# Sliding-window attention and a gated FFN on one core: casts on two engines, fillers for PE, token halves, later loads through POOL's queue

## The chip, the cores and the metric

The kernel runs on one core of a Trainium2 chip. The metric is the device time of one execution in microseconds (us); lower is better. The times below are the median of several executions, and one execution was recorded by the hardware profiler. PE is the matrix engine, DVE the vector engine, ACT the scalar engine, POOL the GpSimd engine, SP the engine that here only issues transfers (DMAs).

## The reference

For each of 8 batches and 8 heads, attention over 576 tokens of 64 numbers with a window of 32 to each side; then an FFN of 512 to 1024 to 512 with a convolution of three taps over the tokens and a gate.

```python
scores = scale * np.matmul(q, k.transpose(0, 1, 3, 2))
mask = np.abs(pos[:, None] - pos[None, :]) <= window          # window = 32
attn = softmax(np.where(mask, scores, -1e9))
x = np.matmul(attn, v)                                        # heads side by side: (8, 576, 512)
h = np.maximum(x @ w_in, 0.0)                                 # (8, 576, 1024)
conv_out = sum(conv_w[k] * h_shifted[k] for k in range(3))
out = (h * sigmoid(conv_out)) @ w_out                         # (8, 576, 512) float32
```

Inputs and output are float32; the kernel computes its products in bfloat16.

## The kernel before

The kernel does not run loops at run time: everything is laid out once as a list of tasks. `Order.add` takes a task with the engines that could do it, what it reads and writes, and a wanted time `t`. `Order.run` is a planner: it keeps a modelled clock for each engine and picks, again and again, the ready task with the smallest `t`; a task with two possible engines goes to the one that the model has done first. It emits each task as it is picked, so each engine's order of instructions is fixed by the planner. The wanted times come from `PARAMS`. PSUM has 8 banks; a task that opens banks waits until the planner finds some free.

The attention goes batch by batch (`loads`, `transposes`, `scores`, `values`, `x_turned`). `loads` brings q and k of a batch in two tiles each (`qkst`, 128 partitions by 1152 numbers) and V in five overlapping blocks (`vst`); POOL casts each to bfloat16 (`qkb`, `ve`), and DVE makes a copy of V shifted by 64 rows (`vo`). There is one set of staging tiles, and two sets of the cast ones. `paced` lets a load of batches 2 to 7 begin only when the load two before it has landed. `transposes` turns q and k on PE, ACT or DVE copy them out of PSUM (`qT`, `kT`); `scores` computes nine tiles of 64 by 128 per head, ACT takes the exponential, DVE multiplies by the mask; `values` multiplies with V and a column of ones, DVE divides by the sum (`rec`, `xn`); `x_turned` transposes the result into `xT`.

The FFN goes by chunks of 384 tokens: 12 chunks, three for each two batches. Chunk 0 lies in batch 0; chunk 1 holds the last 192 tokens of batch 0 and the first 192 of batch 1, and is done in two parts (`part` 0 and 1) so that the first can go ahead of batch 1. `first` is the product with w_in and the relu (`hT`), `moves` shifts slices of `hT` between partitions by SBUF-to-SBUF DMAs into `gT`, `gates` does the convolution by small products with diagonal blocks, tanh on ACT and the gating product on DVE, and `second` is the product with w_out, whose result goes through the tile `wst` to the output. The weights are loaded in float32 into that same tile and cast by POOL.

All loads, moves and stores are issued by SP in one queue, in the planner's order; only the small conv weights come through ACT. The beginning is ordered by wanted times far below zero: q, k and V of batch 0, w_in, q, k and V of batch 1, w_out.

Of the kernel before, what the change touches and what calls it, by code (L numbers as in the profile page):

```python
# [14 lines left out]
RING = 3100  # L15

# [15 lines left out]
class Order:  # L32
# [3 lines left out]
    def __init__(self):  # L36
        self.tasks, self.writer, self.readers = [], {}, {}

    def add(self, kinds, emit, t, reads=(), writes=(), opens=None, ps=(), after=(), claims=()):


        deps = set(after)
# [10 lines left out]
        task = Task(len(self.tasks), kinds, emit, t, deps, opens, ps)  # L53
        task.soft = soft - deps
        for k in reads:
            self.readers.setdefault(k, []).append(task)
# [8 lines left out]
    def run(self, emit=True):  # L65
        free = {"PE": 0.0, "ACT": 2800.0, "DVE": 6000.0, "POOL": 4400.0, "SP": 800.0}
        mode, channel, backlog = None, 0.0, []
        bank_free = [0.0] * 8
# [40 lines left out]
        while pending:  # L109
            best = None  # L110
            for e, xs in ready.items():
# [5 lines left out]
                while pick is None:  # L117
# [18 lines left out]
                    if pick is None:  # L136
                        later = min([later] + [x.ready for x in xs if x.ready > now])
                        if later == float("inf"):
                            break
                        now, held = later, []  # L140
                if pick and (best is None or pick[0] < best[0] - 1e-6):
                    best = (pick[0], e, pick[1], pick[2])
# [3 lines left out]
            if len(x.kinds) > 1:  # L146
                def done(k):
                    return max(free[k], x.ready) + x.kinds[k][1]
                f = min(x.kinds, key=done)
                if f != e:  # L150
                    e, now = f, max(free[f], x.ready)
                    busy, result, more = x.kinds[e]
            if e == "PE":
                if more != mode:
                    busy, result, mode = busy + 90.0, result + 90.0, more
            if e == "SP":
# [6 lines left out]
                channel = max(now + busy + 600.0, channel) + packets * each / 16.0  # L163
                backlog.append((channel, packets))
                result = channel + slack - now
            free[e] = now + busy
# [16 lines left out]
            for y in x.after:  # L183
                if x in y.deps:
                    y.ready = max(y.ready, x.end + (0.0 if e == "SP" else SEM))
# [9 lines left out]
def kernel(  # L195
# [68 lines left out]
    mask = sb([128, 2, S], BF16, "mask")  # L264

# [24 lines left out]
    def pl(n):  # L290
        return 150 + 0.85 * n, 200 + 0.85 * n, None
# [6 lines left out]

    def turn(s):
# [4 lines left out]
    o = Order()  # L304
    nc.scalar.dma_start(conv_w24, moe_conv_w.rearrange("k (m p) -> (k m) p", p=128))
# [32 lines left out]


# [8 lines left out]

    def loads(b):
        i = b % NLD  # L350

        def load_qk(y, j):
            src = (q, k)[y][b, 4 * j:4 * j + 4, :, :]
            sync.dma_start(
                qkst[y][j].rearrange("p e j d -> p e (j d)"),
                bass.AP(src.tensor, src.offset, [[RP * D, 128], [2 * S * D, 2], [1, RP * D]]),
            )

# [3 lines left out]
        def load_v(c):  # L362
            lo = 128 * c - PAD
            s0, s1 = max(0, lo), min(S, lo + 128)
            sync.dma_start(
# [14 lines left out]
        if b < 2:  # L380
            x, dx = (-100.0 if b == 0 else -50.0), 0.1
# [5 lines left out]
        def paced():  # L387
            return before[-2:-1] if b > 1 and len(before) > 1 else []

        for j in range(NPH):  # L390
            for y in range(2):
                t = x + n * dx
                o.add({"SP": dma(256, 110)}, lambda e, y=y, j=j: load_qk(y, j), t,
                      writes=[("st", y, j)], after=paced())
                before.append(o.tasks[-1])
                o.add({"POOL": pl(1152)}, lambda e, y=y, j=j: cast_qk(y, j, e), t,
                      reads=[("st", y, j)], writes=[("b", i, y, j)])
                n += 1
        for c in range(NBLK):
            t = x + n * dx  # L400
            o.add({"SP": dma(1024, 21)}, lambda e, c=c: load_v(c), t, writes=[("vst", c)], after=paced())
            before.append(o.tasks[-1])
            o.add({"POOL": pl(512)}, lambda e, c=c: cast_v(c, e), t,
                  reads=[("vst", c)], writes=[("ve", i, c)])
            n += 1
        for cs in ((0, 2), (2, 4)) if b == 0 else ((0, 4),):
            for half in range(2):
                o.add({"DVE": dve(520 * (cs[1] - cs[0]), 4)},
                      lambda e, cs=cs, half=half: shift(half, cs), x + n * dx,
                      reads=[("ve", i, c + half) for c in range(*cs)],  # L410
                      writes=[("vo", i, c, half) for c in range(*cs)])

    def load_w_in():
        for h in range(2):
# [9 lines left out]
            o.add({"SP": dma(512, 95)}, load, -60.0, writes=[("ws", 4 * h + c) for c in range(4)])  # L424
            for c in range(KC):
                o.add({"POOL": pl(512)}, lambda e, h=h, c=c: cast(e, h, c), -60.0 + h,
                      reads=[("ws", 4 * h + c)], writes=[("w_in", h, c)])

    def load_w_out():
        rows = moe_w_out.rearrange("(h c p) f -> p h c f", c=4, p=128)  # L430
        for c in range(4):
            def load(e, c=c):
                for lo, at, n in turn(c):
# [5 lines left out]
            o.add({"SP": dma(256, 95, len(turn(c)))}, load, -40.0,  # L439
                  writes=[("ws", 4 * h + c) for h in range(2)])  # L440
            for h in range(2):
                o.add({"POOL": pl(512)}, lambda e, h=h, c=c: copy(e, w_out_sb[:, 4 * h + c, :], ws[:, 4 * h + c, :]),
# [18 lines left out]
    def conv_weights():  # L461
        ps = Banks(1)
        o.add({"PE": pe(200.0, "f32")},
              lambda e: tensor.matmul(bank(ps, 0)[:, 0:3 * MB], conv_w24, ident24, start=True, stop=True),
              5.0, opens=ps, writes=[("cw24",)])
        o.add({"DVE": dve(24)}, lambda e: vector.tensor_copy(
            out=conv_w_sb.rearrange("p k m -> p (k m)"), in_=bank(ps, 0)[:, 0:3 * MB]),
            5.0, reads=[("cw24",)], writes=[("cw",)], ps=[ps])
        o.add({"DVE": dve(768)}, lambda e: vector.tensor_tensor(
# [5 lines left out]
    def transposes(g2):  # L475
# [3 lines left out]
        i, n = b % NLD, g2 % NKT  # L479
        for y in range(2):  # L480
# [16 lines left out]
            o.add({"PE": pe(280.0, "rows")}, mm, t + Q["TR"],  # L497
                  reads=[("b", i, y, j)], writes=[("tr", g2, y)], opens=ps,
                  claims=[("T", n, y, h) for h in range(2)])
            for h in range(2):  # L500
                o.add({"ACT": act(576), "DVE": dve(576)},
# [366 lines left out]
```

## Time and profile before

| | |
|---|---|
| three runs | 241.81, 242.25, 245.48 us; median 242.25 |
| the profiled execution | 243.37 us, span from first to last instruction 241.7 us |
| busy: PE, DVE, ACT, POOL | 208.1, 160.1, 164.0, 80.9 us |
| granted clock of PE, mean | 0.972 |
| DMA | 49.62 MB, mean 205 GB/s; the SP queue's packets took 71.6% of 16 engines' span |
| batch 0's first cast of q / first FFN product / first product with w_out | 4.76 / 25.54 / 54.62 us |

The span is what the trace covers; the execution's own time has some 1.7 us around it. Busy time counts an engine's instructions, without its waits and without the issuing of DMAs. A matrix product's recorded time includes its way through the array, so PE's busy share is not its share of peak. Line 274 of the kernel is the helper through which nearly all instructions go, so rows are told apart by their tiles.

### The profile page before, as it was taken

What the parts mean: (1) busy time and instruction counts of PE and PEld (TensorE: products, weight loads), DVE (VectorE), ACT (ScalarE), POOL (GpSimd) and SP (SyncE); (2) the same over time, 40 slices, a digit from 0 to 9 for tenths busy, and PEclk for the clock granted to TensorE, in tenths of its full rate; (3) what the DMA queues carried; (4) which work ended last, traced back from release to release, by engine and by line L of the source; (5) the groups of instructions that cost most, each with busy time, mean ns of one, the idle gap of its engine ahead of it and who ended that gap; (6) DMA issues with size and microseconds to landing.
All of it is one profiled execution on the core that took longest, in us unless ns stands there. A gap on an engine that the chain in (4) does not pass through costs nothing. (4 is left out here: it accounts for less than half of the span.)

```text
span 241.7 us, 9128 instructions
## 1 busy us (share of the span) xinstructions
PE 208.1 (86%) x3878; PEld 124.3 (51%) x3906; DVE 160.1 (66%) x268; ACT 164.0 (68%) x291; POOL 80.9 (33%) x96
## 2 busy tenths in 40 slices
PE   1536995589998869999999998999999999999993
PEld 0425464365655454565455654655555655555541
DVE  7586166998575899546399779698684595524140
ACT  1650586445698576679977886679778885876751
POOL 5757744536613444662236517321000000000000
PEclk9999999758999997999999999999999999999999
DMA  6999999989698899969489989756132223342534
GB/s 237 292 289 392 248 233 223 275 229 337 168 290 186 217 293 355 328 186 278 98 207 356 264 225 281 161 129 205 37 129 55 79 105 68 123 110 54 177 113 181
DMA packets 67228, 49.62 MB, mean 205 GB/s; under 512 B 46172, under 2 KB 52340, under 8 KB 67188
## 3 DMA queue, kind: packets, MB, share of 16 engines
q1 hardware_dynamic: 67152, 49.03, 71.6%
q8 instruction: 30, 0.49, 0.9%
q14 instruction: 10, 0.08, 0.1%
q10 hardware_dynamic: 36, 0.01, 0.0%
HBM read 32.52 MB, written 9.44 MB: 174 GB/s over the span
## 5 line engine op out<-in xcount | busy, mean ns | idle before, releaser
L274 PE MATMUL pst<-xT,w_in_sb 128*128 128x385 bf16 (+2 forms) x416 | 75.4, 322 | 1.6 <-ACT xT L274 0.6
L274 PE MATMUL pst<-w_out_sb,gT 128*128 128x512 bf16 x260 | 64.3, 384 | 3.2 <-issue 2.2
L274 PEld LDWEIGHTS <-w_in_sb 128*128 128x128 bf16 x416 | 37.6, 100 | 25.8 <-issue 3.4
L274 ACT ACTIVATE hT<-pst 128x385 bf16<-128x385 f32 (+2 forms) x80 | 38.6, 489 | 11.1 <-PE pst L274 10.1
L274 DVE SCALAR_TENSOR_TENSOR gT<-tn,gT 128x384 bf16<-128x384 f32 (+2 forms) x52 | 42.4, 842 | 3.9 <-DMA gT<-hT 3.9
L274 POOL CAST ve<-vst 128x512 bf16<-128x512 f32 x40 | 29.4, 741 | 45.7 <-DMA vst<-in_v_dram 43.5
L274 ACT ACTIVATE attn<-pst 128x640 bf16<-128x640 f32 x64 | 39.4, 667 | 4.9 <-PE pst L274 4.9
L274 PEld LDWEIGHTS <-gT 128*128 128x128 bf16 x288 | 26.6, 99 | 31.0 <-issue 3.3
L274 ACT ACTIVATE tn<-pst 128x768 f32<-128x768 f32 (+1 forms) x52 | 37.4, 768 | 6.5 <-PE pst L274 4.6
L274 ACT COPY wst<-pst 128x512 f32<-128x512 f32 x36 | 21.2, 588 | 29.6 <-PE pst L274 28.1
L274 DVE TENSOR_TENSOR attn<-attn,mask 128x1152 bf16<-128x1152 bf16 x32 | 26.9, 846 | 12.3 <-ACT attn L274 12.1
L274 DVE TENSOR_TENSOR xn<-pst,rec 128x640 bf16<-128x640 f32 x32 | 25.8, 818 | 0.5
L274 DVE SCALAR_TENSOR_TENSOR gT<-tn,hT 128x384 bf16<-128x384 f32 (+1 forms) x26 | 14.7, 564 | 16.5 <-ACT tn L274 16.4
L274 POOL CAST qb<-qst 128x1152 bf16<-128x1152 f32 x16 | 19.9, 1242 | 16.2 <-DMA qst<-in_q_dram 12.5
L274 POOL CAST kb<-kst 128x1152 bf16<-128x1152 f32 x16 | 19.9, 1243 | 16.0 <-DMA kst<-in_k_dram 14.3
L274 PE MATMUL pst<-hT,diag_w 32*32 32x384 bf16 (+1 forms) x1248 | 21.2, 322 | 1.8 <-DVE xn L274 1.0
L274 ACT COPY xT<-pst 128x1024 bf16<-128x1024 bf16 (+1 forms) x16 | 11.8, 781 | 13.9 <-PE pst L274 13.9
L274 PEld LDWEIGHTS <-attn 128*64 128x64 bf16 x640 | 14.1, 119 | 13.6 <-issue 8.6
L274 PE MATMUL pst<-ve,attn 128*64 128x65 bf16 x384 | 17.4, 206 | 3.8 <-DVE attn L274 2.3
L274 PE MATMUL pst<-qT,kT 64*128 64x64 bf16 x576 | 17.5, 197 | 3.1 <-DVE kT L274 0.8
L274 PE MATMUL pst<-vo,attn 128*64 128x65 bf16 x256 | 15.6, 206 | 3.3 <-DVE vo L274 3.3
L274 PEld LDWEIGHTS <-kT 64*128 64x128 bf16 x576 | 12.2, 98 | 12.0 <-issue 9.2
(37 smaller groups left out, 163.4 us busy)
## 6 DMA issues: line engine op xcount, KB each, us to landing
qst<-in_q_dram SPq DMA_DIRECT2D x16, 576.0 KB, 6.4
kst<-in_k_dram SPq DMA_DIRECT2D x16, 576.0 KB, 7.3
out_dram<-wst SPq DMA_DIRECT2D x11, 768.0 KB, 5.8
vst<-in_v_dram SPq DMA_DIRECT2D x24, 256.0 KB, 5.5
vst<-in_v_dram SPq DMA_DIRECT2D x16, 192.0 KB, 5.9
wst<-in_moe_w_in_dram SPq DMA_DIRECT2D x2, 1024.0 KB, 7.9
gT<-hT SPq DMA_DIRECT2D x14, 144.0 KB, 3.6
gT<-hT SPq DMA_DIRECT2D x34, 48.0 KB, 2.1
```

What stands on the lines that cost most here:

```text
L274: return lambda *args, **kwargs: fixed(do(*args, **kwargs))
```

## The change

- Casts of q, k, V, w_in and w_out may go to POOL or ACT; the planner picks whichever it has done first. In the planner POOL's casts, DVE's masks, shifts and gating products share a modelled port, so that it does not lay them over one another.
- Fillers: where the planner sees a gap ahead of a PE task before 62 us, `warm` issues products of a constant tile into PSUM bank 7, as many as fit; bank 7 is held back from other use until then.
- Token halves: batch 0 is loaded, cast, transposed, scored (tiles 0 to 3, then 4 to 8), masked, multiplied with V (blocks 0 and 1, then 2 to 4) and turned in two halves of tokens, and chunk 0 of the FFN is done in two parts. The order of loads becomes: first half of q and k (k through ACT's queue), V blocks 0 to 2, half of w_in, second half of q and k, V blocks 3 and 4, the other half of w_in, batch 1, w_out.
- q, k and V of batches 2 to 7 are issued by POOL, and `paced` looks four loads back.
- The planner's numbers (`PARAMS`) are other ones, and each task's wanted time gets an offset from a table (`NUDGE`, by kind of task and batch or chunk), so the order of the instructions is another one throughout.

The core of the diff:

```diff
     def run(self, emit=True):
...
+        bank_free = [0.0] * 7 + [WARM]
...
+            if e == "POOL" and isinstance(more, tuple):
+                packets, each, slack = more
+                second = max(now + busy + 1000.0, second, channel) + packets * each / 16.0
+                result = second + slack - now
...
+            if e == "PE" and emit and now < WARM:
+                gap, each = (now - free[e], 260.0) if free[e] else (now - 4000.0, 430.0)
+                self.warm(int((gap - 300.0) / each))
...
+    def load(b, packets, ns):
+        return {"POOL": (1000.0, None, (packets, ns, 1300.0))} if b > 1 else {"SP": dma(packets, ns)}
...
+    def warm(n):
+        for i in range(n):
+            tensor.matmul(pst[:, 7, :], warm_sb[:, 0:128], warm_sb, start=True, stop=True)
...
         def load_qk(y, j):
             src = (q, k)[y][b, 4 * j:4 * j + 4, :, :]
-            sync.dma_start(
+            (pool if b > 1 else sync).dma_start(
...
+        def load_half(y, j, half):
+            for e_ in range(2):
+                src = (q, k)[y][b, 4 * j + 2 * e_:4 * j + 2 * e_ + 2, 32 * RP * half:32 * RP * half + 32 * RP, :]
+                (scalar if y and not half else sync).dma_start(
+                    qkst[y][j][64 * e_:64 * e_ + 64, half, :, :].rearrange("p j d -> p (j d)"),
+                    bass.AP(src.tensor, src.offset, [[RP * D, 32], [S * D, 2], [1, RP * D]]),
+                )
...
         def paced():
-            return before[-2:-1] if b > 1 and len(before) > 1 else []
+            return before[-4:-3] if b > 1 and len(before) > 3 else []
...
-                o.add({"POOL": pl(1152)}, lambda e, y=y, j=j: cast_qk(y, j, e), t,
-                      reads=[("st", y, j)], writes=[("b", i, y, j)])
+                o.add("qc", {"POOL": pl(1152), "ACT": act(1152)}, lambda e, y=y, j=j: cast_qk(y, j, e), t,
+                      reads=[("st", y, j)], writes=[("b", i, y, j)] + [("b0", y, j, h) for h in halves0])
...
-        for i in range(NP):
-            values(b * NP + i)
+        for part in (0, 1) if b == 0 else (None,):
+            for i in range(NP):
+                values(b * NP + i, part)
```

296 lines of the change are left out of this document (205 added, 91 removed), and 79 rows, old and new, of tables (NUDGE, PARAMS).

## The prediction

> **What bounds the kernel now.** I began with the page: span, busy shares, and the row of PE in forty slices.
>
> ```profile
> span 241.7 us, 9128 instructions
> PE 208.1 (86%) x3878; PEld 124.3 (51%) x3906; DVE 160.1 (66%) x268; ACT 164.0 (68%) x291; POOL 80.9 (33%) x96
> PE   1536995589998869999999998999999999999993
> ```
>
> PE is thin in the first eight or nine slices and nearly full behind them. So the second view was the busy time by stage (stage, its length, busy us of PE, PEld, DVE, ACT, POOL, granted clock, DMA share, GB/s), cut at the first FFN matmul, at the two stretches with a lower clock, at the last loads and at the tail.
>
> ```profile
> 0.00:25.50 25.50, 10.83 (x246) 8.83 (x246) 17.75 (x43) 9.57 (x15) 17.40 (x27) 1.00 1.01 307
> 25.50:45.40 19.90, 15.91 (x344) 10.47 (x344) 11.06 (x21) 13.44 (x25) 11.40 (x16) 1.00 0.99 221
> 45.40:52.40 7.00, 4.49 (x108) 3.53 (x108) 6.71 (x12) 1.62 (x3) 2.41 (x2) 0.50 0.86 260
> 52.40:55.60 3.20, 3.20 (x62) 1.96 (x60) 2.39 (x8) 2.48 (x5) 1.22 (x2) 0.50 0.95 331
> 55.60:80.00 24.40, 22.80 (x496) 13.91 (x499) 17.78 (x27) 19.34 (x39) 10.92 (x12) 1.00 0.90 238
> 80.00:89.70 9.70, 6.86 (x185) 4.53 (x184) 9.03 (x15) 6.42 (x12) 4.47 (x5) 1.00 0.88 251
> 89.70:93.20 3.50, 3.17 (x24) 2.11 (x23) 3.44 (x4) 2.47 (x3) 2.09 (x3) 0.51 1.08 371
> 93.20:160.00 66.80, 64.42 (x1208) 37.29 (x1216) 47.94 (x77) 51.47 (x93) 28.38 (x30) 1.00 0.88 241
> 160.00:230.00 70.00, 68.63 (x1139) 38.15 (x1150) 41.79 (x68) 52.79 (x94) 2.58 (x3) 1.00 0.34 102
> 230.00:241.70 11.70, 7.82 (x81) 3.52 (x80) 2.24 (x4) 4.44 (x7) 0.00 (x0) 1.00 0.40 148
> ```
>
> Length minus PE busy gives PE's idle time: 14.7 + 4.0 + 2.5 = 21.2 us before 52.4, then 1.6, 2.8, 0.3, 2.4 and 1.4, and 3.9 in the tail: 33.6 in all. Three things follow. From 93.2 to 230 PE is busy 133.1 of 136.8 us: little is to be had there, and only by taking PE away from its work could it get worse. Before 52.4 PE does not bound; the DMA engines are full (1.01, 0.99) and DVE is. And between 80 and 89.7 DVE is busy 9.03 of 9.70 us while PE idles.
>
> The third view was the order of time around the early steps.
>
> ```profile
> 25.54 4.12 PE L274 MATMUL pst<-xT,w_in_sb 128*128 128x385 bf16 x16 [0.55 <-ACT xT L274]
> 27.74 0.15 PEld L274 LDWEIGHTS <-w_in_sb 128*128 128x128 bf16 x1 [0.17 <-issue]
> 28.06 1.20 PEld L274 LDWEIGHTS <-w_in_sb 128*128 128x128 bf16 x7 [0.17 <-issue]
> 18.90 2.29 POOL L274 CAST w_in_sb<-wst 128x512 bf16<-128x512 f32 x4 [1.43 <-DMA wst<-in_moe_w_in_dram]
> 34.57 0.62 POOL L274 CAST ve<-vst 128x512 bf16<-128x512 f32 x1 [1.53 <-DMA vst<-in_v_dram]
> 40.23 1.03 DVE L274 COPY vo<-ve 64x2080 bf16<-64x2080 bf16 x1
> 42.16 1.11 DVE L274 COPY vo<-ve 64x2080 bf16<-64x2080 bf16 x1
> 44.28 0.21 DVE L274 RECIPROCAL rec<-pst 128x10 f32<-128x10 f32 x1
> 44.52 0.82 DVE L274 TENSOR_TENSOR xn<-pst,rec 128x640 bf16<-128x640 f32 x1
> 49.78 1.67 PE L274 MATMUL pst<-ident,xn 128*128 128x128 bf16 x14 [0.85 <-DVE xn L274]
> 50.63 1.01 ACT L274 COPY xT<-pst 128x1024 bf16<-128x1024 bf16 x1 [4.80 <-PE pst L274]
> 52.46 1.48 PE L274 MATMUL pst<-xT,w_in_sb 128*128 128x193 bf16 x8
> 54.62 2.37 PE L274 MATMUL pst<-w_out_sb,gT 128*128 128x512 bf16 x7
> ```
>
> The first FFN matmul starts at 25.54. Weight loads of this group come 0.32 us apart at 27.74 and 1.20 / 7 = 0.17 apart from 28.06, so the array ran at half pace until then although the clock column says 1.00; I count all that lies before 28.06 as half pace. The landmark I use is 52.46, where chunk 1's second half, the first work that needs batch 1, reaches PE; behind it PE does not stop for long. Batch 1's last V block was cast at 34.57, 17.9 us earlier. The work between is short; it waits in DVE's queue behind the FFN of chunk 0 (the shifts start at 40.23 and 42.16).
>
> **The change part by part.**
>
> *Token halves, and casts on two engines.* Less has to land before the first FFN matmul: half of q and k, three of five V blocks and the first half of w_in are 1.2 + 0.7 + 1.0 MB where 3.5 + 1.0 MB landed by 18.90. At that pace (18.90 us less about 2 of start) it lands at 2 + 16.9 x 2.9 / 4.5 = 12.9; four casts by two engines take 1.2 us, so I expect the first FFN matmul near 16, with the first quarter of the work only. That alone moves nothing at the end: it clears chunk 0 from DVE and ACT before batch 1 arrives. The bytes ahead of batch 1's last V are the same, so it still lands near 34.5. From there: cast 0.6, two shifts 2.1, values about 0.5, four normalisations 4 x (0.21 + 0.82) = 4.1, turning 1.7, copy 1.0: 44.5. The landmark moves from 52.46 to between 44.5 and 52.46. I take 44.5, because chunk 0 is out of the way by then: gain **7.9**, bounds 0 and 8.
>
> The halves add instructions: eight extra issues on SP and four on ACT, 72 more transposes, four more masks, reciprocals and normalisations, eight more activations. At 0.2 to 0.5 us each these are some 3 us on DVE and 3 on ACT; in 0.00:25.50 these have 7.8 and 15.9 us free. Nothing is charged; without that cover it would be 3 us.
>
> *Work pulled forward.* The first w_out product starts at 54.62. With the chunk-0 gates done early, some of its 5 us can fill PE before the landmark, but only as w_out's casts allow:
>
> ```profile
> 42.11 3.27 POOL L274 CAST w_out_sb<-wst 128x512 bf16<-128x512 f32 x4 [1.39 <-DMA wst<-in_moe_w_out_dram]
> ```
>
> They end at 45.4 and cannot end much sooner with the DMA engines full. Gain 0 to 3, taken as **2**.
>
> *Fillers.* They occupy PE only in planned gaps up to 62 us, from a tile that nothing else uses. What they buy behind the landmark is the half clock of 52.40:55.60: PE was busy all 3.20 us at 0.50, so **1.6**. Before the landmark a faster array shortens only parts of a chain set by loads and DVE; I add nothing. Their price: one PSUM bank less until 62 us and a filler that runs past its gap, 0.43 us each by 512 columns at the pace above (0.32 us for 385). 0 to 2, taken as **-0.5**, one filler.
>
> *Between 80 and 93.2* PE loses 2.8 + 0.3 idle and 1.6 by the 0.51 clock. DVE limits there, and no DVE work is removed after batch 0. Another order may spread it: 0 to 4, taken as **1.5**.
>
> *Loads of batches 2 to 7 through POOL, four in flight.* Three rows bound what an issue costs.
>
> ```profile
> 52.11 0.46 SPq L274 DMA_DIRECT2D vst<-in_v_dram  x1
> 0.80 0.65 ACTq L305 DMA_DIRECT2D conv_w<-in_moe_conv_w_dram  x1
> 16.63 13.35 SPq L274 DMA_DIRECT2D vst<-in_v_dram  x5
> 165.46 0.82 POOL L274 CAST ve<-vst 128x512 bf16<-128x512 f32 x1 [2.02 <-DMA vst<-in_v_dram]
> 42.72 0.55 SPq L274 DMA_DIRECT2D qst<-in_q_dram  x1
> L274 POOL CAST ve<-vst 128x512 bf16<-128x512 f32 x40 | 29.4, 741 | 45.7 <-DMA vst<-in_v_dram 43.5 <-PE pst L274 1.3 <-DVE attn L274 0.7
> L274 POOL CAST kb<-kst 128x1152 bf16<-128x1152 f32 x16 | 19.9, 1243 | 16.0 <-DMA kst<-in_k_dram 14.3 <-PE pst L274 1.5
> L274 POOL CAST qb<-qst 128x1152 bf16<-128x1152 f32 x16 | 19.9, 1242 | 16.2 <-DMA qst<-in_q_dram 12.5 <-PE pst L274 3.7
> ```
>
> A V block's issue took 0.46 us when nothing held it, ACT's only one 0.65, and 13.35 / 5 = 2.67 where a full queue held it. The trace has no issue by POOL. I take 1.0, near the low rows because four in flight do not fill a queue; bounds 0.46 and 2.67. The loads of six batches span 42.72 to 165.46, 20.5 us a batch, or some 18.8 when 10 us are saved. POOL's casts are 2 x 1.243 + 2 x 1.242 + 5 x 0.741 = 8.7 us a batch; nine issues at 1.0 make 17.7, and 12.5 with 60% of the casts. It fits. Queued behind a POOL issue that waits for an earlier load stand POOL's casts, and behind these the transposes; that is where the price would show.
>
> What leaves SP's queue frees the 102 moves from gT to hT. But the waits of PE after 60 us show that they hardly cost it anything:
>
> ```profile
> PE pst L274 <- ACT attn L274: 0.8, 4, 0.3
> PE pst L274 <- ACT qT L274: 0.7, 2, 0.5
> PE pst L274 <- DMA gT<-hT: 0.3, 2, 0.2
> ```
>
> So 0.3 us at most; no gain. ACT's share of the casts does cost. POOL's casts after 55.6 are 48.4 us; 40% of them are 19 us on ACT, busy 79.7 of 104.4 us in 55.60:160.00 (the sum of four rows): 95%. PE's waits for ACT above are 1.5 us; I let them double, **-1.5**, bounds 0 and -5.
>
> *Sum.* 7.9 + 2 + 1.6 - 0.5 + 1.5 - 1.5 = 11.0 us. The profiled execution took 243.37 us in all, span 241.7; less 11 that is 232.4. The three runs have a median of 242.25, 1.1 below it, so the forecast is 231.3, said as **231**.
>
> **The rivals.**
>
> *A smaller gain: the landmark stays.* DVE is busy 6.71 of 7.00 us in 45.40:52.40, and if its order keeps chunk 0 ahead of the normalisations, only clock and pulled-forward work remain: 1.6 + 2 - 0.5 - 1.5 = 1.6, that is 240.6; with half the move 4 less, 236.7. Against it: chunk 0's matmuls have their data some 9 us earlier.
>
> *A larger gain.* Time lost to idling and half pace in 0 to 93.2 is 21.2 + 4.7 + (13.6 + 4.5 + 3.2 + 3.2) / 2 = 38 us, the brackets being PE's busy time before 28.3, in the two early stages at 0.50 and in 89.70:93.20. If PE, warm from the start, does w_out work before the landmark and loses nothing between 80 and 93, add 1 more of w_out, the other 3.2 of the 4.7 us between 80 and 93.2, the 1.5 charged to ACT, and 4 us for the idle time of 25.50:45.40: 231 - 9.7 = 221.
>
> *Slower: POOL becomes the bound.* One mechanism: an issue on POOL costs so much that nine of them and the casts left on it outlast a batch's 18.8 us. With 60% of the casts, 9i + 5.2 > 18.8, that is i > 1.5 us. At i = 2.0 each batch is 4.4 us late, 26 over six; some 8 of it I take as covered by loads that run ahead (batch 2's first load was issued at 42.72, 9.7 us before the landmark), so 18 remain: 231 + 18 = 249. The 2.67 row speaks for it, the 0.46 and 0.65 rows against.
>
> The Trainium skill (SBUF — State Buffer, "The 'DVE blocks DMA' trap") gives a reason for that rival: descriptors of a DMA issued from POOL are written by POOL's cores, which a DVE copy in a two-port mode locks out, and it advises the other queues. By that rule, DVE's two shifts of a batch (1.03 and 1.11 us above) would lengthen POOL's batch by at most 2.1 us, and the rival would decide from i = 1.3. The trace agrees that the two exclude each other:
>
> ```profile
> 90.80 1.15 POOL L274 CAST qb<-qst 128x1152 bf16<-128x1152 f32 x1 [0.73 <-DMA qst<-in_q_dram]
> 90.90 1.59 DVE L274 COPY vo<-ve 64x2080 bf16<-64x2080 bf16 x1
> ```
>
> A shift that takes 1.03 us at 40.23 took 1.59 here, ending 0.5 us behind the cast that began before it.
>
> *The change does not do what it says.* Fillers end at planned 62 us, so a gap like 80 to 89.7 still halves the clock; this is inside the 1.5 above.
>
> **How the numbers follow.** Forecast 231 (224 to 236, by half the move on one side and most of the larger gain on the other): 0.50. Larger gain (below 224, centre 221): 0.24. Smaller gain (236 to 247): 0.15, of which 0.04 lies below 237.4. Slower (249): 0.11. 2% of 242.25 is 4.8 us, about what can be told from no change: faster means below 237.4, slower above 247.1. Faster: 0.50 + 0.24 + 0.04 = 0.78; within: 0.11; slower: 0.11. The range goes down to 217 (the larger gain's 221 less the 4 us of the ACT bound and a filler) and up to 243, where the landmark stays and ACT costs 4 instead of 1.5; it leaves out the slower case and some hundredths on each side.
>
> **What would show it.** Right: the first w_in matmul near 16, chunk 1's second half on PE near 44.5, clock 1.0 around 50 to 56, about 54 issues on POOL near 1 us, ACT above 85% and PE above 95% between 55 and 160, an unchanged tail. Wrong: the landmark beyond 50; POOL's issues above 1.5 us with PE waiting for qb, kb or ve; or PE idle behind ACT by more than 5 us.

## The result: slower by 4.3%, and the profile after

The changed kernel takes 253.57 us (four runs, 253.34 to 253.59) against 243.8 us before (four runs beside it, 241.81 to 245.48): a ratio of 1.0427, 95% interval 1.0324 to 1.053. The forecast of 231 us has the wrong sign, and its range of 217 to 243 does not hold the time. Some executions of a kernel run longer, mostly at a lower granted clock; all ratios here leave them out, so a ratio can differ from that of two medians, and of the four kernels profiled in such an execution only the times are used (before_pool, replanned_sp, sp_casts_pool) and ACT's busy time (before_shared_casts).

The page of the changed kernel, to be laid beside the rows of before: busy time, PE in forty slices, and the two DMA queues (packets, MB, share of 16 engines).

```profile
span 251.8 us, 9463 instructions
PE 221.4 (88%) x4025; PEld 129.2 (51%) x4060; DVE 174.2 (69%) x320; ACT 184.4 (73%) x314; POOL 74.6 (30%) x100
PE   4978898577999988999859989999999999999993
q1 hardware_dynamic: 32368, 27.21, 39.5%
q0 software_dynamic: 5664, 21.24, 30.2%
```

PE is busy from the first slice on: 14.7 us of its 221.4 are fillers. The thin places are now slices 8 to 10 and 21 (6.3 us each). The same by stage:

```profile
25.50:45.40 19.90, 17.51 (x354) 12.89 (x356) 16.25 (x37) 17.39 (x31) 8.90 (x13) 0.91 1.10 297
45.40:55.60 10.20, 6.45 (x162) 4.09 (x165) 7.82 (x15) 6.80 (x11) 7.31 (x9) 0.83 1.05 244
55.60:80.00 24.40, 21.29 (x480) 13.55 (x486) 18.44 (x35) 20.98 (x42) 7.80 (x10) 1.00 0.97 249
80.00:93.20 13.20, 11.58 (x260) 7.05 (x261) 12.75 (x23) 12.16 (x21) 5.89 (x9) 1.00 1.01 318
93.20:160.00 66.80, 59.40 (x1114) 33.26 (x1123) 52.89 (x86) 51.13 (x84) 32.92 (x40) 0.95 0.78 210
160.00:230.00 70.00, 68.78 (x1189) 39.01 (x1197) 48.54 (x82) 53.34 (x93) 2.61 (x3) 1.00 0.33 96
230.00:251.80 21.80, 17.69 (x173) 8.34 (x173) 5.22 (x8) 9.50 (x16) 0.00 (x0) 1.00 0.46 166
```

Behind 160 us PE is nearly full in both kernels and does the same work, so the time is decided by what is left to do at that point: 68.78 + 17.69 = 86.5 us of PE here, 68.63 + 7.82 = 76.4 before. Those 10 us are the result. They were lost in two places. Counting PE's busy time without fillers from a moment to the end, as windows cut there give it, the changed kernel is 2.4 us behind at 40 us, 6.9 at 60, still 6.6 at 120, and 10.0 at 160. So there is an early loss, up to 60, and a late one, mainly between 120 and 140; and 80 to 93.2 did improve, as forecast (PE 11.58 us against 6.86 + 3.17, clock 1.00).

Between 120 and 140 PE is busy 15.38 us where it was 19.18 before. Most of these 3.8 us are one wait, in slice 21: DVE waits for a move, and PE for the normalisation queued behind it.

```profile
130.72 0.96 DVE L300 SCALAR_TENSOR_TENSOR gT<-tn,gT 128x768 bf16<-128x768 f32 x1 [3.20 <-DMA gT<-hT]
132.46 0.19 PE L300 MATMUL pst<-ve,attn 128*64 128x65 bf16 x1 [3.29 <-DVE xn L300]
```

The moves issued in 110 to 131 take 7.6 us to land at the median; before, those issued in 100 to 125 take 3.5.

The order of time in the early steps: the first FFN product and the last of its chunk-0 stretch, batch 2's first cast of q, batch 1's last V cast and last normalisations, the landmark, w_out's last cast and first product.

```profile
21.26 1.49 PE L300 MATMUL pst<-xT,w_in_sb 128*128 128x193 bf16 x16 [0.38 <-DVE xT L300]
44.05 0.49 PE L300 MATMUL pst<-xT,w_in_sb 128*128 128x192 bf16 x4 [0.19 <-DVE hT L300]
41.84 1.16 ACT L300 CAST qb<-qst 128x1152 bf16<-128x1152 f32 x1
45.33 0.66 ACT L300 CAST ve<-vst 128x512 bf16<-128x512 f32 x1
55.25 1.49 DVE L300 TENSOR_TENSOR xn<-pst,rec 128x640 bf16<-128x640 f32 x2
60.63 2.84 PE L300 MATMUL pst<-xT,w_in_sb 128*128 128x193 bf16 x32
62.74 0.61 ACT L300 CAST w_out_sb<-wst 128x512 bf16<-128x512 f32 x1
72.28 1.67 PE L300 MATMUL pst<-w_out_sb,gT 128*128 128x512 bf16 x7 [0.16 <-issue]
```

The first product is earlier (25.54 before), but what the forecast wanted earlier behind it is later: the landmark at 60.63 instead of 52.46 (forecast 44.5), batch 1's last V cast at 45.33 instead of 34.57, w_out's first product at 72.28 instead of 54.62. Of the 10.8 us by which that V cast is late, 5.6 are the load's: in the traces the last packet of this V ends at 39.35, and at 33.79 before. The rest is ACT's queue: ACT works without a gap from 38.40 to 48.07, and batch 2's cast of q at 41.84 stands ahead of batch 1's V. The DMA rows show what stands ahead of the load; first two of the loads that POOL issues, then the moves in 30 to 62 us, after and before.

```profile
30.02 0.84 POOL L300 DMA_DIRECT2D qst<-in_q_dram  x1 [3.27 <-ACT qb L300]
35.67 0.72 POOL L300 DMA_DIRECT2D qst<-in_q_dram  x1 [1.11 <-ACT kT L300]
L300 SPq DMA_DIRECT2D gT<-hT x8: 590/612/691, 40.3 to 59.8; - x8
DMA to landing us min/median/max: 7.3/13.3/17.6
L274 SPq DMA_DIRECT2D gT<-hT x13: 602/636/697, 34.6 to 62.0; - x13
DMA to landing us min/median/max: 3.1/6.0/9.5
```

Batch 2's q and k are issued from 30.02, while SP is still issuing batch 1's V (21.64 to 34.9) and then w_out (35.0 to 39.3). Before, one queue held them until 42.72, behind w_out. And the moves of these stages take 13.3 us to land where they took 6.0.

### The profile page after: what moved, and what is told of

The parts are those of the page before. It is cut to its first block, busy times and chain, and to the rows that moved or that the text cites. A ratio compares the mean times of both kernels' runs of the same rounds, so it can differ in the third digit from the quotient of the medians.

```text
span 251.8 us, 9463 instructions
## 1 busy us (share of the span) xinstructions
PE 221.4 (88%) x4025; PEld 129.2 (51%) x4060; DVE 174.2 (69%) x320; ACT 184.4 (73%) x314; POOL 74.6 (30%) x100
## 3 DMA queue, kind: packets, MB, share of 16 engines
q0 software_dynamic: 5664, 21.24, 30.2%
## 4 chain that ended last, share of the span: by engine, by line
PE 42%; DMA 8%; DVE 6%; issue 3%; ACT 2%; SPq 1%; DVEq 0%; ACTq 0%
PE pst L300 42%; DMA gT<-hT 8%; DVE gT L300 2%; SPq L300 1%; DVE xn L300 1%; DVE vo L300 1%; ACT tn L300 1%; DVE xT L300 1%; DVE hT L300 1%; ACT kb L300 0%; ACT hT L300 0%; DVE qT L300 0%; ACT wst L300 0%; ACT ve L300 0%; DVE rec L300 0%
## 5 line engine op out<-in xcount | busy, mean ns | idle before, releaser
L300 PE MATMUL pst<-xT,w_in_sb 128*128 128x385 bf16 (+3 forms) x448 | 75.0, 314 | 1.8 <-DVE xT L300 1.0
L300 ACT ACTIVATE hT<-pst 128x385 bf16<-128x385 f32 (+3 forms) x69 | 31.4, 464 | 17.1 <-PE pst L300 16.7
L300 ACT ACTIVATE attn<-pst 128x640 bf16<-128x640 f32 (+1 forms) x64 | 39.0, 662 | 5.6 <-PE pst L300 5.4
L300 DVE TENSOR_TENSOR attn<-attn,mask 128x1152 bf16<-128x1152 bf16 (+2 forms) x36 | 27.9, 784 | 12.5 <-ACT attn L300 12.3
L300 DVE TENSOR_SCALAR hT<-pst 128x385 bf16<-128x385 f32 (+3 forms) x43 | 19.9, 476 | 19.5 <-PE pst L300 15.7
L300 POOL DMA_DIRECT2D vst<-in_v_dram x30 | 26.0, 868 | 21.7 <-ACT ve L300 17.8
L300 DVE TENSOR_TENSOR xn<-pst,rec 128x640 bf16<-128x640 f32 (+2 forms) x36 | 26.0, 739 | 0.4
L300 PEld LDWEIGHTS <-diag_w 32*32 32x32 bf16 x1248 | 12.6, 88 | 14.3 <-issue 11.6
L300 ACT COPY qT<-pst 128x576 bf16<-128x576 bf16 x20 | 12.7, 653 | 6.9 <-PE pst L300 6.8
L300 PE MATMUL pst<-warm 128*128 128x512 bf16 x41 | 14.7, 488 | 2.7 <-issue 2.7
```

Of the source, the lines that this page charges most:

```text
L300: return lambda *args, **kwargs: fixed(do(*args, **kwargs))
```

## The experiments

`before` was run beside each kernel; ratios are to it, with 95% intervals. Kernels that were not run beside one another are best compared by these ratios.

**Each part alone.** These say most, so they come first.

before_shared_casts: each cast may go to POOL or ACT.

```diff
-o.add({"POOL": pl(1152)}, lambda e, y=y, j=j: cast_qk(y, j, e), t,
+o.add({"POOL": pl(1152), "ACT": act(1152)}, lambda e, y=y, j=j: cast_qk(y, j, e), t,
```

(V, w_in and w_out alike.)

> The kernel before, in which the planner may give each cast to POOL or ACT, and nothing else. If sharing the casts is harmless by itself: within 2 us of before (241 to 246). Rival (casts on ACT stand ahead of exponentials and relus on an engine that is 68% busy): 247 to 252, with ACT above 175 us busy and more PE waits for ACT than before.

244.08 us, ratio 0.9997 (0.9935 to 1.0058): nothing, although ACT's busy time rose from 164.0 to 180.6 us. Sharing the casts, planned for this order, costs nothing that can be told and buys nothing either.

before_fillers: the fillers, with bank 7 held back until the planned 62 us.

```diff
-bank_free = [0.0] * 8
+bank_free = [0.0] * 7 + [WARM]
...
+if e == "PE" and emit and now < WARM:
+    gap, each = (now - free[e], 260.0) if free[e] else (now - 4000.0, 430.0)
+    self.warm(int((gap - 300.0) / each))
```

> The kernel before, with the fillers and with bank 7 held back until the planned 62 us, planned anew by the old wanted times; no halves, no shared casts, all loads on SP. If the fillers by themselves are worth something and the bank costs little: faster than before by 1 to 3 us (240 to 241). Rival (holding back one of eight banks, or fillers that run past their gap, delays work that ends late): 245 or more, with the loss already there at 62 us.

246.73 us, 1.0162 (1.0079 to 1.0245): slower by more than its interval, if by less than 2%, and the rival's sign. The clock did what was wanted (0.993 instead of 0.972 on average, and 1.00 in 45.4 to 60 instead of 0.65), and no time came of it. The first FFN product comes at 29.27 instead of 25.54, and at 60 us PE has 5.6 us more work left than before. Whether the bank or the fillers did that was not separated.

halves_alone: of the changed kernel only the token halves, with the order of the first loads that goes with them; casts on POOL, no fillers, eight banks, loads on SP, the old numbers, no modelled port and no offsets.

```diff
-(pool if b > 1 else sync).dma_start(
+sync.dma_start(
...
-{"POOL": pl(1152), "ACT": act(1152)}
+{"POOL": pl(1152)}
...
-for i in range(n):
+for i in range(0):
...
-self.nudge, self.index = NUDGE, 0
+self.nudge, self.index = {}, 0
```

> Of the change only the token halves of batch 0 (and chunk 0 in two parts): all casts on POOL, no fillers, eight banks, all loads on SP, the old planner numbers and no offsets; planned anew. If the halves are worth what the forecast took them for: first FFN product near 19 as without fillers, chunk 1's second half on PE below 48 (52.46 before), time 236 to 240. Rival (the landmark is set by batch 1's bytes and by DVE's queue, so the halves move nothing behind it, and their extra issues and small instructions cost): landmark 52 to 56, 243 to 250.

249.66 us, 1.0327 (1.0222 to 1.0433): the rival again, with a landmark even later than it said, at 63.67. The order of time of this kernel: the first FFN products, the casts of the second half of w_in, the two shifts of batch 1's V, the last FFN products ahead of batch 1, and the first of chunk 1's second half.

```profile
19.81 1.45 PE L300 MATMUL pst<-xT,w_in_sb 128*128 128x193 bf16 x8 [0.78 <-DVE xT L300]
24.50 2.97 POOL L300 CAST w_in_sb<-wst 128x512 bf16<-128x512 f32 x4 [1.84 <-DMA wst<-in_moe_w_in_dram]
44.29 0.70 DVE L300 COPY vo<-ve 64x2080 bf16<-64x2080 bf16 x1
45.69 1.14 DVE L300 COPY vo<-ve 64x2080 bf16<-64x2080 bf16 x1
48.30 1.89 PE L300 MATMUL pst<-xT,w_in_sb 128*128 128x193 bf16 x12 [3.44 <-issue]
63.67 1.17 PE L300 MATMUL pst<-xT,w_in_sb 128*128 128x193 bf16 x12
```

The first product comes 5.7 us earlier than before, but the second half of w_in is cast only by 27.47 (23.92 before), the FFN work ahead of batch 1 ends later (at 50.2 instead of 42.1), and the shifts that stood at 40.23 and 42.16 stand at 44.29 and 45.69. At 60 us PE has 6.7 us more work left than before, and 7.3 at 160, so the loss is made early. How much of it is w_in's late half is not shown: 3.44 of the 8.1 us are PE's wait at 48.30, for which the profile names no cause. What is shown is that the first piece came early, the last piece late, and that nothing was won by the first.

before_pool: the kernel before with only the queue of the loads of batches 2 to 7 changed; every engine keeps its order. It was run twice, the second time as before_pool_again.

```diff
-sync.dma_start(
+(pool if b > 1 else sync).dma_start(
```

> The kernel before with only this: q, k and V of batches 2 to 7 issued by POOL in the place that the planner gave them; PE, DVE and ACT in the same order. Here batch 2's loads stand behind w_out's casts on POOL, so nothing early is overtaken. Theory 1: the moves land later (median of the 96 KB ones 4 us or more where 3.4 stood) and the time rises by 2 to 7 us, 246 to 251. Theory 2: 242 to 245, no change.

> The kernel before with q, k and V of batches 2 to 7 issued by POOL and nothing else, a second time. Theory A: 249 to 252, with moves and w_out landing later than in before (w_out 9.2 us there). Rival (the issues and waits on POOL, not the sharing, cost): the same time, but moves and w_out land as before, and the waits of PE are for casts.

252.12 us, 1.0302 (1.0191 to 1.0412), and 256.45 us, 1.0583 (1.0483 to 1.0683). Each is a loss of the kind that the whole change made (4.3%). Their sizes differ, but the first kernel's four times spread from 247.98 to 262.15 us and hold all four of the second's, 254.60 to 258.19. Because the order is the same, the same instruction can be followed through both traces (the second run's is used). SP's issues of the second and the fifth output store, before and then with POOL's queue:

```profile
83.97 0.80 SPq L274 DMA_DIRECT2D out_dram<-wst  x1
141.61 1.23 SPq L274 DMA_DIRECT2D out_dram<-wst  x1
...
85.46 0.40 SPq L274 DMA_DIRECT2D out_dram<-wst  x1
156.83 0.38 SPq L274 DMA_DIRECT2D out_dram<-wst  x1
```

The delay is 1.5 us at the second store and 15.2 at the fifth; the next two are 14.6 and 14.9 late. DVE's instructions show where it grows: those between 86 and 89 are 2.8 us late, and two waits add 3.0 us near 92 and 4.8 near 137. The gating product, the normalisation and PE around the first wait, before (two rows; PE's transposes follow at 89.15, 0.78 us idle) and then with POOL's queue, one product with the mask behind it, and the second wait:

```profile
86.58 1.78 DVE L274 SCALAR_TENSOR_TENSOR gT<-tn,gT 128x768 bf16<-128x768 f32 x1
88.28 0.81 DVE L274 TENSOR_TENSOR xn<-pst,rec 128x640 bf16<-128x640 f32 x1
...
92.43 2.41 DVE L274 SCALAR_TENSOR_TENSOR gT<-tn,gT 128x768 bf16<-128x768 f32 x1 [2.97 <-DMA gT<-hT]
94.76 0.81 DVE L274 TENSOR_TENSOR xn<-pst,rec 128x640 bf16<-128x640 f32 x1
95.63 0.67 PE L274 MATMUL pst<-ident,qb 64*128 64x64 bf16 x18 [3.73 <-DVE xn L274]
102.72 2.34 DVE L274 TENSOR_TENSOR attn<-attn,mask 128x1152 bf16<-128x1152 bf16 x1
137.43 0.96 DVE L274 SCALAR_TENSOR_TENSOR gT<-tn,gT 128x768 bf16<-128x768 f32 x1 [4.81 <-DMA gT<-hT]
```

DVE waits for a move, the normalisation queued behind it is late, and PE stands. The two waits are 7.8 us of the 15. Another 3.5 us lie between 92 and 105 in DVE's own instructions, which take longer beside a POOL that now works without a pause: the product with the mask at 102.72 takes 2.34 us where it took 0.74 before, with two POOL casts from 102.74 to 104.45. The last six moves ahead of the second store, issued in 73 to 84 before and in 76 to 84 with POOL's queue:

```profile
DMA to landing us min/median/max: 3.0/4.0/5.1
DMA to landing us min/median/max: 3.2/9.6/11.6
```

The expectation of the second run had w_out land later, too. It does not: 7.6 us at the median against 8.6 before.

before_pool_two: a real limit of two loads in flight on POOL. (`paced` is none: it sets the planner's ready times, and nothing on the chip waits by it.)

```diff
+def behind(tile_):
+    if len(sent) > 1:
+        pool.tensor_copy(out=seen[0:sent[-2].shape[0], 0:1], in_=sent[-2])
+    sent.append(tile_)
```

> before_pool with a real limit of two loads in flight on POOL's queue: ahead of each issue POOL reads one number a partition of the tile loaded two before, so it waits until that load has landed. Theory A (loads that POOL sends without a limit fill the DMA engines together and moves land late): the wait of DVE for a move near 92 (2.97 us) and 137 (4.81 us) goes, and the time falls from 252 to 256 to below 250. Rival B (the queue costs for another reason, or POOL standing on a landing holds its casts): 252 or more, and POOL's casts come later than without the limit.

272.76 us, 1.1302 (1.1205 to 1.1399). The first half of theory A is shown, and the time is rival B's. The same six moves' landing in this kernel, and its waits (us, times, longest):

```profile
DMA to landing us min/median/max: 3.7/4.3/5.3
DVE vo L274 <- POOL ve L274: 25.2, 11, 8.8
POOL seen L274 <- DMA qst<-in_q_dram: 12.0, 8, 3.1
```

With two in flight the moves land in 4.3 us again, and DVE's waits for moves are 3.8 us in all, as before (3.9) and not 12.2. So it was POOL's loads in flight that made the moves late, though the DMA engines also had less to do here (a share of 0.55 in 76 to 92, 0.91 in both other kernels). But POOL, standing on landings, holds its own casts, and DVE now waits 25.2 us for them. In one SP queue the loads were held back without any compute engine standing.

**Undoing parts of the changed kernel.** loads_on_sp and loads_on_act change only the queue, not the planned order.

```diff
-(pool if b > 1 else sync).dma_start(
+sync.dma_start(                              # loads_on_sp
+(scalar if b > 1 else sync).dma_start(       # loads_on_act
```

> The changed kernel with the loads of batches 2 to 7 issued by SP again, each in the place that the planner gave it; the order of PE, DVE and ACT is the same to the instruction. Theory 1 (a second queue takes the order away: POOL's loads share the DMA engines with what is urgent, first batch 1's V and w_out, later the moves from hT to gT): batch 2's q and k still stand ahead of w_out in SP's list, so the early delay goes only in part, but the moves land sooner; 243 to 250 us, moves on the chain of waits clearly below 7.9%. Theory 2 (the new order and the casts on ACT are what costs, whichever queue loads): 252 to 256. Theory 3 (the fillers hold PE back early): 252 to 256.

> The changed kernel with the loads of batches 2 to 7 issued through ACT's queue in place of POOL's, each in its planned place. A second queue again, but a hardware one, so its packets are as small as SP's. Theory (POOL's queue moves bigger packets, and a move waits for one between each two of its own): the moves land in some 3 us where POOL's loads made them 4 to 5, and the stretch 93 to 160 recovers; total 248 to 252 unless ACT waits to issue. Rival (any second queue takes the engines' time from the moves): moves land as late as with POOL, 252 to 258.

loads_on_sp takes 249.87 us (249.01 to 250.11), 1.0304 (1.0252 to 1.0357), and loads_on_act, with two runs, 261.82 us, 1.0851 (1.0688 to 1.1015). SP's queue takes 3.7 us off the changed kernel by the times and 1.2% (some 3 us) by the ratios, whose intervals just overlap. By the traces it is gained late: PE's work left is nearly the same up to 120 us (120.3 against 121.0) and 2.9 us less at 160, and moves in 30 to 62 land in 4.9 us instead of 13.3. Not all of the late loss is the queue's: DVE still waits 2.64 us for a move at 133.35. The early loss stays in loads_on_sp, where w_out's last cast is at 63.5.

ACT's queue costs 8 us more than POOL's by the times and some 10 by the ratios, but not by late moves. Their landing in 30 to 62 in loads_on_act, and ACT behind its issue of a V block of batch 2 at 47.04:

```profile
DMA to landing us min/median/max: 4.1/5.8/6.9
47.42 1.15 ACT L300 CAST qb<-qst 128x1152 bf16<-128x1152 f32 x1 [5.55 <-DMA wst<-in_moe_w_out_dram]
```

The moves land nearly as with SP's queue, and over all 102 none takes more than 7.0 us (17.6 in the changed kernel). So a second queue need not make the moves late; in these kernels POOL's did. It brought its 21.24 MB in 5664 packets, where ACT's queue carried 21.84 MB in 35012: the expectation's theory, that a move waits for POOL's large packets, fits the landing, but no run changes the packets alone. The time went elsewhere: ACT stands 5.55 us ahead of that issue, and 2.29 and 3.68 us ahead of the next ones at 50.94 and 56.13, with exponentials and tanh queued behind them.

no_fillers, fillers_capped (4 instead of 18 fillers in the first gap), no_nudges and whole_loads (batch 0's q and k in 8 transfers, not 16):

```diff
-for i in range(n):
+for i in range(0):                           # no_fillers
+n = n if done_ else min(n, 4)                # fillers_capped, in warm
-self.nudge, self.index = NUDGE, 0
+self.nudge, self.index = {}, 0               # no_nudges
+if half:                                     # whole_loads, in load_half:
+    return                                   # the first call brings both halves
```

> The changed kernel without the filler products, all else in the same order. Theory 1: fillers are not the cause; within 2 us of the changed kernel (252 to 256), with the first FFN product hardly sooner than 21.3 and lower granted clock early. Theory 3: fillers push real work on PE, so without them the landmark (chunk 1's second half) comes sooner and the time is 243 to 248.

> The changed kernel with 4 fillers in the first gap in place of 18. There they hold PE from 4.3 to 11.2 us, while q's first half is cast at 5.9. Theory (the first batch of fillers overruns its gap): first transposes near 6.5, first FFN product 18 to 20 where it is 21.3, but PE is cold until some 14 us; the loads set the rest, total 251 to 254. Rival (early start carries through): 247 to 250.

> The changed kernel with the table of offsets empty, so the planner orders all tasks by its own wanted times; POOL's queue, casts, fillers and halves stay. Theory A (the offsets put the order wrong: batch 2's loads and casts ahead of batch 1's end): 240 to 248. Theory B (the loss is in the parts, not in the offsets): 252 to 262.

> The changed kernel with batch 0's q and k in four pairs of transfers of both halves at the beginning (8 issues, not 16); nothing waits for less, every engine but SP and ACT's queue keeps its order. Theory (the small half transfers slow the load stream: 4.6 MB by 20 us where the kernel before had 5.7): batch 1's V starts some 3 us sooner, first FFN product later by 2 to 3, total 250 to 253. Rival (halves earn what they cost): 253 to 256.

In this order: 256.5 us, 1.0558 (1.0462 to 1.0654); 253.02, 1.0402 (1.0242 to 1.0562); 259.71, 1.0735 (1.0666 to 1.0805); 260.92, 1.076 (1.0673 to 1.0848). Within the changed kernel's order the offsets save some 6 us and the split transfers 7, more than either theory on them had. The fillers seem to save 3, but their interval overlaps the changed kernel's (1.0324 to 1.053). The cap on the fillers changes nothing that can be told.

**Batch 2 ahead of batch 1's end.** In the changed order batch 2's q and k come early on every engine. sp_wout_first holds these loads back behind w_out's, on SP, with the engines' order kept; b2_casts_pool also puts their casts on POOL; sp_casts_pool and wout_first_casts_pool put all casts on POOL, without and with the holding back.

```diff
+if b == 2 and not flushed:                   # sp_wout_first, in load_qk
+    held.append((load_qk, y, j))
+    return
...
+copy("POOL" if b == 2 else e, qkb[i][y][j]...)   # b2_casts_pool, in cast_qk
```

> As loads_on_sp, but batch 2's q and k are held back until SP has issued w_out; PE, DVE, ACT and POOL keep the changed kernel's order. It isolates the overtaking early on. Theory 1 (loads of batch 2 overtake batch 1's V and w_out): w_out's last cast some 5 us sooner than in loads_on_sp and the total 3 to 6 us below it, 244 to 247. Rival (the fixed order of casts and attention behind it sets the pace, whichever load comes first): within 1.5 us of loads_on_sp, 248.5 to 251.5.

> As sp_wout_first, where ACT stood still 7.2 us before a cast of batch 2's q that had not landed, with batch 1's exponentials queued behind it; here batch 2's four q and k casts run on POOL instead, all else the same. Theory (the fixed order needs batch 2's loads early because ACT's queue holds their casts ahead of urgent work; feed them early and they overtake w_out, feed them late and ACT stalls): ACT's stall goes, chunk 1's second half reaches PE near 52 to 55 where it was 61.8, total 244 to 249. Rival (the stall only moves to the next wait in the fixed order): landmark still beyond 58, total 251 to 256.

> As loads_on_sp, but every cast runs on POOL, in the place in time that the planner gave it; ACT's order is the same without its 58 casts, PE and DVE unchanged. Theory: casts on ACT stand in front of the exponentials and relus of an engine that PE waits for, so taking them off gives 2 to 5 us: 245 to 248. Rival: POOL now has some 80 us of casts in one queue behind one another, late loads block it, and the time rises to 251 to 255. If neither, within 1.5 us of 249.9.

> As sp_wout_first, with every cast on POOL, so no load is waited for on ACT at all. Theory: like b2_casts_pool in the early part and, with 20 us less on ACT later, 241 to 247, near the kernel before. Rival (POOL's single queue of casts, in an order made for two engines, blocks): 250 to 256.

In the order named: 254.71 us, 1.0535 (1.0425 to 1.0645); 253.44, 1.0475 (1.0372 to 1.0578); 251.54, 1.0379 (1.0302 to 1.0456); 257.59, 1.0557 (1.0442 to 1.0672). None gains on loads_on_sp, and no theory that hoped for a gain holds: in sp_wout_first w_out's last cast still starts at 64.0, and in b2_casts_pool the landmark comes at 65.57. The traces of the first two say why, ACT in the one and POOL in the other:

```profile
48.29 1.15 ACT L300 CAST qb<-qst 128x1152 bf16<-128x1152 f32 x1 [7.18 <-DMA qst<-in_q_dram]
49.35 0.59 ACT L300 ACTIVATE attn<-pst 128x512 bf16<-128x512 f32 x1
...
49.59 1.15 POOL L300 CAST qb<-qst 128x1152 bf16<-128x1152 f32 x1 [13.57 <-DMA qst<-in_q_dram]
```

Batch 2's cast stands in the engine's queue ahead of batch 1's exponentials. If its load comes early, it takes the DMA engines from batch 1's V and w_out (in loads_on_sp, with one queue, the last packet of that V ends at 42.27, later than in the changed kernel); if it is held back, the engine stands 7.18 us (13.57 on POOL) with batch 1's work behind it. The queue can't mend what the order asks for.

So two kernels were planned anew: replanned_sp with all loads on SP, and b2_behind_wout with batch 2's nine loads on SP behind w_out's.

```diff
-    return {"POOL": ...} if b > 1 else {"SP": dma(packets, ns)}
+    return {"POOL": ...} if b > 99 else {"SP": dma(packets, ns)}   # replanned_sp
+    return {"POOL": ...} if b > 2 else {"SP": dma(packets, ns)}    # b2_behind_wout
...
-line=lead if b < 2 else None
+line=lead if b < 3 else None                                       # b2_behind_wout
```

> The changed kernel with the loads of batches 2 to 7 on SP both in the planner and in fact, so the order is planned anew: w_out ahead of batch 2's loads. Casts on two engines, fillers, halves and offsets stay. Theory 1: w_out's product starts some 10 us sooner than 72.3, total 236 to 246. Theory 2: 250 to 258, since the casts on ACT and the offsets stay.

> The changed kernel, planned anew with batch 2's nine loads issued by SP behind w_out's loads (batches 3 to 7 stay on POOL). Theory A (in the changed kernel batch 2's loads run beside batch 1's last V and w_out and delay the two, and that early delay is never made up): w_out's last cast falls from 62.74 to below 52, chunk 1's second half reaches PE below 55 and the time falls to 246 to 249. Rival B (the new order as a whole is what costs, wherever batch 2's loads stand): the landmark stays near 60 and the time within 2 us of 253.6 or above it.

261.57 us, 1.0752 (1.0663 to 1.0841), slower than either theory had it, and 269.04 us, 1.1064 (1.0967 to 1.116). In b2_behind_wout theory A is right on its steps and rival B on the time. Chunk 1's second half, w_out's casts on POOL, and ACT's longest later wait:

```profile
53.80 2.37 PE L300 MATMUL pst<-xT,w_in_sb 128*128 128x193 bf16 x16
48.15 0.61 POOL L300 CAST w_out_sb<-wst 128x512 bf16<-128x512 f32 x1 [1.49 <-DMA wst<-in_moe_w_out_dram]
68.78 0.62 ACT L300 CAST ve<-vst 128x512 bf16<-128x512 f32 x1 [6.15 <-DMA vst<-in_v_dram]
```

The landmark returns from 60.63 to 53.80 and w_out's last cast from 62.74 to 48.15. So it was batch 2, ahead of batch 1's end, that made both late; how much of it by loads and how much by casts is not told, since the plan moves both. But batch 2's V now comes late, its cast holds ACT 6.15 us with a tanh behind it, and the kernel ends 15 us later than the changed one. In both, the old wanted times and offsets with other arrivals made an order worse than either kernel's. No kernel here was measurably faster than the one before.

## Why the prediction was wrong

**The halves (gain 7.9): the step "chunk 0 is out of the way by then" failed.** The first product came at 21.26 (forecast near 16), and with the halves alone at 19.81; but the FFN work that follows ends later, at 44.54 instead of 42.1 (50.2 in halves_alone), and the second half of w_in is cast from 25.08 on instead of 21.63. By itself this part costs 3.3%. I had looked at when the first piece can start and not at when the last can end.

**"The bytes ahead of batch 1's last V are the same, so it still lands near 34.5": failed.** Its last packet ended 5.6 us later than before and it was cast at 45.33. The forecast kept the old list of bytes and did not ask where the new wanted times put batch 2's loads and casts. It was not the second queue as such: in loads_on_sp three of batch 2's loads are issued by SP itself ahead of the last two V blocks, and the V is later still. And from that cast to the landmark it took 15.3 us where the forecast added up 10.0.

**Loads through POOL (costed at nothing): the price was looked for in the wrong place.** The estimate of an issue, 1.0 us, was close:

```profile
L300 POOL DMA_DIRECT2D vst<-in_v_dram x30 | 26.0, 868 | 21.7 <-ACT ve L300 17.8 <-DVE rec L300 1.8 <-POOL ve L300 1.5
```

0.87 us for a V block and 0.71 for k, and POOL is busy 30% of the span. POOL does not bound; the slower rival had the sign and not the mechanism. Nor was there a limit of four in flight to lean on, since `paced` sets only the planner's ready times. What POOL's queue costs is a move that in SP's one queue stood ahead of later loads and now lands among them, and a POOL that keeps DVE waiting. By itself that is 3.0 to 5.8%; in the changed kernel it has a part in the wait at 130.72.

The Trainium skill (DMA: Bandwidth & Descriptors, "Issuing engines are not separate DMA queues") states that transfers started by different engines run on the same 16 DMA engines and interleave. The traces agree, with 9.6 us to land a move instead of 4.0 where POOL issues the loads, though with ACT issuing them the moves land hardly later than with SP.

The rule of the Trainium skill that the forecast cited (SBUF — State Buffer, "The 'DVE blocks DMA' trap") does not show in the issues: POOL's longest took 1.07 us. That POOL and DVE exclude each other shows in DVE instead, in the 2.34 us above.

**"0.3 us at most" for the moves: a bound taken from the wrong kernel.** PE's wait of 0.3 us for moves was measured with the loads in SP's queue, and as PE's own wait. The moves reach PE through DVE's gating product and the normalisation behind it; that wait, 3.9 us in all before, is 12.2 in before_pool_again.

**w_out's work pulled forward (gain 2): the opposite,** 72.28 instead of 54.62. w_out's last cast came at 62.74 (44.8 before).

**Fillers (gain 1.6 less 0.5):** the clock rose and no time came of it; alone they cost 1.6%. In the changed order they cost nothing and may save 3 us, so their worth hangs on the order. **Casts (cost 1.5):** alone nothing measurable (0.0%, 0.6% each way), so too high there; ACT was busy 84.3 of 104.4 us in 55.6 to 160, 81% and not the 95% that was added up (and PE 92.3, 88%, where above 95% was to be the sign). What they cost in the changed order was not separated, but batch 1's last V cast waited in ACT's queue there. **80 to 93.2 (gain 1.5):** right, 11.58 against 10.03 us of PE, and given back three times over in 93.2 to 160, where PE is busy 59.40 instead of 64.42 us. I had called that stretch one with little to gain and not asked what it could lose.

**What stays open.** The parts alone cost 0.0, 1.6, 3.3 and 3.0 to 5.8%; together 4.3%, less than their sum. How the 4.3% divides inside the new order the runs do not say: undoing the queue gives back some 3 to 4 us of the 10, and every other undoing made it worse or changed nothing that can be told. No kernel has the new numbers and offsets without the parts. The halves and fillers were planned anew with wanted times made for another set of parts, so their prices alone contain some price of the order. In before_pool the order is the same and its price is the queue's; between 3.0 and 5.8% its size is uncertain.

## What to carry to other kernels

A single in-order DMA queue is also a priority list: before loads are given a queue of their own, list the small transfers that now stand ahead of them and what waits for these. Here the moves took more than twice as long to land in the busy stretches beside POOL's loads (9.6 us instead of 4.0, 13.3 instead of 6.0), and hardly longer beside ACT's. Splitting work into halves is worth what the last half gains, not the first. Where each engine's order is fixed in advance, a transfer made later by some 5 us changes which engine stands, so price a change of arrivals by the in-order queue behind each cast.

## What the runs showed of the hardware

In the changed kernel an issue on POOL took 0.70 to 1.07 us; the same loads' issues on ACT took 0.38 at the median. A read of one number a partition on POOL took some 0.3 us. With the loads in POOL's queue the moves of a busy stretch took 9.6 us to land instead of 4.0, though over all 102 moves the median rose only from 3.0 to 3.6 and the DMA engines were not busier (65.7% of the span against 71.6%). A limit of two loads in flight restored the landing (4.3 us), but the kernel took 16 us more than without it. A product with the mask on DVE took 2.34 us instead of 0.74 beside two casts on POOL. And a clock of 0.993 instead of 0.972 gained no time.

PE stood several times for nothing that the profile names: 3.44 us ahead of 48.30 in halves_alone, 1.85, 1.71 and 1.29 us in the changed kernel, 2.17 us before. These are all such waits over 0.5 us in the three traces, and each ends 1.2 to 1.6 us behind the end of a 16 KB packet of the DMA queue that the profile calls "instruction". Most such packets pass without a wait. That PE waits there for its instructions to be loaded fits this, but no run tests it.
